# GpSimd's sums of exponentials and its low parts of q and k, issued as two instructions each instead of one

## The chip, the cores and the metric

The kernel runs on one core of one Trainium2 chip. Times are device microseconds of one launch; the kernel before has a median of 662.14 us over three runs (657.9, 662.14 and 665.37 us). The engines are called PE (TensorE), DVE (VectorE), ACT (ScalarE), POOL (GpSimd) and SP (SyncE).

## The reference, cut to what matters

Three layers follow one another: attention in which a query sees only the keys of its own cluster, a mixture of experts with two experts per token, and a soft mixture of experts. The change touches the first.

```python
def _attn_ref(q, k, v, centroids):          # q, k, v: (2, 8, 768, 64)
    ...
    mask = q_assign[:, :, :, None] == k_assign[:, :, None, :]
    scores = scale * np.matmul(q, k.transpose(0, 1, 3, 2))
    scores = np.where(mask, scores, -1000000000.0)
    scores = scores - np.max(scores, axis=-1, keepdims=True)
    attn = np.exp(scores)
    attn = attn / (np.sum(attn, axis=-1, keepdims=True) + 1e-09)
    return np.matmul(attn, v).astype(np.float32)

def reference(**kwargs):
    attn_out = _attn_ref(**attn_kwargs)
    x = np.ascontiguousarray(attn_out.transpose(0, 2, 1, 3)).reshape(B * S, H * D)
    x = _moe_ref(x=x, **moe_kwargs)
    return _moe2_ref(x=x, **moe2_kwargs)
```

## The kernel before, in words

**Pairs and steps.** The 16 heads are worked off as 8 pairs (p = 0 to 7), the two heads of a pair side by side. A pair has 12 steps: two halves of the 768 queries (qh), and for each six blocks of 128 keys (kc). Step (p, t) has qh = t // 6 and kc = t % 6. `score` (L363) makes the scores of 128 keys against 384 queries for both heads in a PSUM tile `psc` of two buffers, and ACT writes their exponentials to a tile `pt` (128 x 2 x 384, L375) of which there are five buffers. `av` (L378) multiplies `pt` with the values into `pav`.

**The sums of exponentials.** The denominators need the sum of the six `pt` tiles of one (p, qh). `add` (L388) gives it out: POOL sums the first n tiles into `psa` (n = 6 in pair 0, 4 in pairs 1 to 5, 3 in pairs 6 and 7), DVE sums the others into `psb`. The first sum reads two `pt` tiles (L402), each later one reads `psa` or `psb` and one `pt` tile (L405). One instruction covers 128 partitions x 768 elements. `total` (L407) adds `psb` to `psa` on DVE for the first three pairs (L411), `den` (L424) sums over the partitions on PE (`pden`), and DVE takes the reciprocals. A `pt` buffer is free for a later step when `av` and the sum have read it.

**High and low parts.** q and k are split into a high part in fp32r and a low part, and the scores are two matmuls, one on the high parts with the mask rows (`BK`, `BQ`) and one on the mixed parts (`AK`, `AQ`). ACT writes the high parts (`hk`, `hq`, `ak`, `aq`), POOL the low parts: `akl` (L301) once for each head, `aql` (L310) once for each half of the queries, 64 partitions x 768 elements each.

**Row maxima.** Before pair p is scored, `munit` (L317) computes its score tiles on PE into `pmx` (two buffers of PSUM) and DVE reduces each to row maxima `mp` (L336, L341); `mfin` (L343) gathers them.

**What sets the order.** `body` walks the steps two at a time and issues, in this order, what the tables `pre`, `mid` and `post` hold for a step: munits and the scores, the high parts, `av` and `add`, then the low parts, the cluster masks (`masks`, L222; L228 is its comparison on DVE), `total`, `den` and `xout` (L441). Between them `gap` issues the routing of finished tokens to the experts: chains of small DVE instructions on tiles of 128 x 48 or 128 x 24 (all under L563, the line of a helper) and then, on POOL, indirect DMAs that scatter token rows to `xg` in memory (L631). Towards the end of attention the first weights of the experts are split too, on DVE (L832) and POOL (L834), and their first tokens (L895). Each engine works its instructions off in the order in which they were issued.

**The other layers** (from about 255 us on) use POOL for scatters and splits of their own and are not touched by the change.

Of the kernel before, what the change touches and what calls it, by code (L numbers as in the profile page):

```python
# [12 lines left out]
OP = mybir.AluOpType  # L13
# [3 lines left out]
B, H, S, D = 2, 8, 768, 64  # L17
# [62 lines left out]
f32 = lambda t: t.bitcast(F32)  # L80


class Attention:
# [216 lines left out]

    def akl(self, p, hh):  # L301
        i = p % 2
        self.nc.gpsimd.tensor_tensor(self.AK[i][0:64, hh], self.raws[p][1][0:64, hh],
                                     f32(self.BK[i])[0:64, hh], op=OP.subtract)

    def aq(self, p, qh):
        q = self.raws[p][0][0:64].rearrange("p h (t n) -> p h t n", t=2)[:, :, qh]
# [2 lines left out]
    def aql(self, p, qh):  # L310
        i = p % 2
        q = self.raws[p][0][0:64].rearrange("p h (t n) -> p h t n", t=2)[:, :, qh]
        self.nc.gpsimd.tensor_tensor(self.AQ[i][64:128, qh], q, f32(self.BQ[i])[0:64, qh], op=OP.subtract)

    MU = 9

# [71 lines left out]
    def add(self, p, t):  # L388

        qh, kc = divmod(t, 6)  # L390
        pt = self.ptile
        n = 6 if p == 0 else 4 if p < MASKED else 3
        first = 0 if kc < n else n
        if kc == first:
            return
        eng = self.nc.vector if first else self.nc.gpsimd
        if kc == first + 1:
            k = "b" if first else "a"
            s = (self.g.at if first else self.g.xp).tile([128, 2, 384], F32, name=f"ps{k}", tag=f"ps{k}",
                                                         bufs=1 if first else 2)  # L400
            self.stile[p, qh, k] = s
            eng.tensor_tensor(s, pt.pop((p, t - 1)), pt.pop((p, t)), op=OP.add)  # L402
        else:
            s = self.stile[p, qh, "b" if first else "a"]
            eng.tensor_tensor(s, s, pt.pop((p, t)), op=OP.add)  # L405

    def total(self, p, qh):  # L407
        if (p, qh, "b") not in self.stile or p >= TWO:
# [1277 lines left out]
```

## Time and profile before

| | us |
|---|---|
| median of 3 runs | 662.14 |
| lowest and highest run | 657.9, 665.37 |
| profiled execution, its own time | 660.52 |
| its span, first to last instruction | 658.7 |
| PE busy | 623.3 (95%) |
| DVE busy | 414.6 (63%) |
| ACT busy | 312.4 (47%) |
| POOL busy | 292.6 (44%) |

The span is 1.8 us shorter than the execution's own time, and that execution lies 1.6 us under the median. Starts in the trace are counted from the span's start. In a row of a timeline a number in square brackets is how long the engine stood idle just before, and behind the arrow stands whose end it waited for. An instruction's duration includes the time for which it was held after its start.

### The profile page before, as it was taken

What the parts mean: (1) busy time and instruction counts of PE and PEld (TensorE: products, weight loads), DVE (VectorE), ACT (ScalarE), POOL (GpSimd) and SP (SyncE); (2) the same over time, 40 slices, a digit from 0 to 9 for tenths busy, and PEclk for the clock granted to TensorE, in tenths of its full rate; (3) what the DMA queues carried; (4) which work ended last, traced back from release to release, by engine and by line L of the source; (5) the groups of instructions that cost most, each with busy time, mean ns of one, the idle gap of its engine ahead of it and who ended that gap; (6) DMA issues with size and microseconds to landing.
All of it is one profiled execution on the core that took longest, in us unless ns stands there. A gap on an engine that the chain in (4) does not pass through costs nothing. (4 is left out here: it accounts for less than half of the span.)

```text
span 658.7 us, 10980 instructions
## 1 busy us (share of the span) xinstructions
PE 623.3 (95%) x3957; PEld 478.9 (73%) x3957; DVE 414.6 (63%) x872; ACT 312.4 (47%) x445; POOL 292.6 (44%) x256
## 2 busy tenths in 40 slices
PE   7899999999798999796999999999999999997996
PEld 5566666676565667685888888888888898885544
DVE  6777889779775698855655455454454556645633
ACT  5577585665457472343334334343434446543102
POOL 4899586864668792582123133251323403101100
PEclk9599999999799999987999999999999999999999
DMA  8393754836436413478574829969796758998995
GB/s 312 76 263 116 250 177 138 282 119 212 147 135 234 130 65 129 161 220 220 129 190 112 221 97 271 314 206 240 284 278 261 163 179 249 348 313 284 378 392 194
DMA packets 63098, 139.80 MB, mean 212 GB/s; under 512 B 15232, under 2 KB 30912, under 8 KB 60992
## 3 DMA queue, kind: packets, MB, share of 16 engines
q1 hardware_dynamic: 57040, 125.38, 56.9%
q0 software_dynamic: 6000, 13.68, 9.5%
q8 instruction: 32, 0.52, 0.3%
q14 instruction: 26, 0.21, 0.1%
HBM read 108.25 MB, written 28.68 MB: 208 GB/s over the span
## 5 line engine op out<-in xcount | busy, mean ns | idle before, releaser
L967 PE MATMUL py<-ring,H 128*128 128x512 f32 (+1 forms) x686 | 175.1, 400 | 6.1 <-DVE H L935 6.1
L832 DVE TENSOR_TENSOR ring<-wr,ring 128x1024 fp32r<-128x1024 f32 (+1 forms) x77 | 92.4, 1200 | 100.3 <-ACT ring L825 99.3
L967 PEld LDWEIGHTS py<-ring,H 128*128 128x128 f32 (+1 forms) x686 | 126.3, 188 | 33.1 <-DVE H L935 6.7
L825 ACT ACTIVATE ring<-wr 128x1024 fp32r<-128x1024 f32 x77 | 81.5, 1058 | 94.5 <-PE py L967 86.4
L375 ACT ACTIVATE pt<-psc 128x768 f32<-128x768 f32 x96 | 77.2, 810 | 71.0 <-PE psc L372 65.1
L975 POOL DMA_INDIRECT x2acc<-y,mdi x31 | 49.9, 1609 | 103.8 <-ACT y L999 98.0
L385 PE MATMUL pav<-pt,vt 128*64 128x384 f32 x384 | 75.2, 514 | 0.0
L336 DVE TENSOR_REDUCE mp<-pmx 128x1 f32<-128x512 f32 x96 | 63.2, 675 | 17.7 <-PE pmx L331 16.9
L932 ACT ACTIVATE H<-ph 128x256 fp32r<-128x256 f32 (+3 forms) x80 | 37.5, 468 | 71.9 <-PE ph L926 66.3
L926 PE MATMUL ph<-XS1a,ring 128*128 128x448 f32 (+2 forms) x288 | 70.4, 335 | 0.0
L926 PE MATMUL ph<-XS0a,ring 128*128 128x448 f32 (+3 forms) x252 | 64.6, 337 | 1.6 <-DVE ring L832 1.4
L405 POOL TENSOR_TENSOR psa<-psa,pt 128x768 f32<-128x768 f32 x32 | 62.0, 1936 | 3.5 <-ACT pt L375 1.4
L935 DVE SCALAR_TENSOR_TENSOR H<-ph,H 128x384 fp32r<-128x384 f32 (+1 forms) x120 | 44.4, 397 | 21.8 <-ACT H L932 20.2
L926 PEld LDWEIGHTS ph<-XS1a,ring 128*128 128x128 f32 x288 | 48.7, 189 | 4.0
L926 PE MATMUL ph<-XS0b,ring 128*128 128x256 f32 (+3 forms) x192 | 48.3, 329 | 0.0
L926 PEld LDWEIGHTS ph<-XS0a,ring 128*128 128x128 f32 x252 | 43.4, 188 | 6.3 <-DVE ring L832 1.9
L926 PE MATMUL ph<-XS1b,ring 128*128 128x256 f32 (+2 forms) x192 | 47.6, 322 | 0.3 <-DVE XS1b L895 0.3
L895 POOL TENSOR_TENSOR XS0b<-xr,XS0a 128x512 fp32r<-128x512 f32 (+1 forms) x9 | 16.8, 1871 | 64.5 <-ACT XS0a L889 64.5
L385 PEld LDWEIGHTS pav<-pt,vt 128*64 128x64 f32 x384 | 23.9, 139 | 25.6 <-issue 20.4
L331 PE MATMUL pmx<-even 96*128 96x512 f32 (+1 forms) x96 | 34.6, 420 | 5.4 <-DVE mp L336 4.5
L631 POOL DMA_INDIRECT xg<-x,idx x24 | 27.2, 1133 | 23.6 <-DVE inv L563 17.8
L341 DVE TENSOR_REDUCE mp<-pmx 128x2 f32<-128x512 f32 x48 | 32.9, 688 | 5.4 <-PE pmx L331 5.0
(335 smaller groups left out, 1030.8 us busy)
## 6 DMA issues: line engine op xcount, KB each, us to landing
wr<-in_w SPq DMA_DIRECT2D x80, 512.0 KB
v<-in_v SPq DMA_DIRECT2D x9, 2048.0 KB
xg<-xr SPq DMA_DIRECT2D x14, 512.0 KB
wr<-in_qk SPq DMA_DIRECT2D x8, 768.0 KB
early<-in_q SPq DMA_DIRECT2D x8, 768.0 KB
early<-in_k SPq DMA_DIRECT2D x8, 768.0 KB
x2acc<-xr SPq DMA_DIRECT2D x8, 512.0 KB
vt<-in_v SPq DMA_DIRECT2D x8, 384.0 KB
```

The lines of the kernel that those rows point to most:

```text
L331: nc.tensor.matmul(o, self.BQ[i][:96, qh, hh, 128 * c:128 * c + 128], self.BK[i][:96, hh, ks], start=True, stop=True)
L336: nc.vector.tensor_reduce(mp[:, 0, col:col + 1], ps, axis=AX.X, op=OP.max)
L375: nc.scalar.activation(pt, ps[:, :, :384], AF.Exp, scale=SCALE)
L385: nc.tensor.matmul(self.avp[p, qh][64 * hh:64 * hh + 64, :384], self.vt[p][:, hh, kc, :], pt[:, hh, :], start=(kc == 0), stop=(kc == 5))
L405: eng.tensor_tensor(s, s, pt.pop((p, t)), op=OP.add)
L825: self.nc.scalar.activation(self.ring[s][0], self.wr[s], AF.Copy)
L832: nc.vector.tensor_tensor(lo[:, :n], wr[:, :n], f32(hi)[:, :n], op=OP.subtract)
L926: nc.tensor.matmul(ph[:, :n], a[:, 128 * c:128 * c + 128], x[:, c, :], start=(c == 0 and i == 0), stop=(c == 3 and i == 2))
L932: nc.scalar.activation(HH, ph[:, :n], AF.Relu)
L935: nc.vector.scalar_tensor_tensor(o, ph[:, a:b], 0.0, f32(HH)[:, a:b], op0=OP.max, op1=OP.subtract)
L967: nc.tensor.matmul(o, x, y, start=(f == 0 and i == 0), stop=(f == NF - 1 and i == 2))
L975: st = nc.gpsimd.indirect_dma_start(out=out, out_offset=bass.IndirectOffsetOnAxis(ap=di, axis=0), in_=y, in_offset=None, compute_op=OP.add)
```

## The change

Every POOL instruction of the three functions is issued as two of half the length. A sum into `psa` is one instruction for each head (128 x 384), where it was one for both. `aql` is likewise one for each head (64 x 384). `akl`, which was for one head already, is cut at key 384. DVE's sums into `psb` stay whole. The sums have a line of their own afterwards, L414; the low parts are L305 and L316.

```diff
     def akl(self, p, hh):
         i = p % 2
-        self.nc.gpsimd.tensor_tensor(self.AK[i][0:64, hh], self.raws[p][1][0:64, hh],
-                                     f32(self.BK[i])[0:64, hh], op=OP.subtract)
+        for n in range(0, S, 384):
+            c = slice(n, n + 384)
+            self.nc.gpsimd.tensor_tensor(self.AK[i][0:64, hh, c], self.raws[p][1][0:64, hh, c],
+                                         f32(self.BK[i])[0:64, hh, c], op=OP.subtract)
...
     def aql(self, p, qh):
...
-        self.nc.gpsimd.tensor_tensor(self.AQ[i][64:128, qh], q, f32(self.BQ[i])[0:64, qh], op=OP.subtract)
+        for h in range(2):
+            self.nc.gpsimd.tensor_tensor(self.AQ[i][64:128, qh, h], q[:, h], f32(self.BQ[i])[0:64, qh, h], op=OP.subtract)
...
             self.stile[p, qh, k] = s
-            eng.tensor_tensor(s, pt.pop((p, t - 1)), pt.pop((p, t)), op=OP.add)
+            x, y = pt.pop((p, t - 1)), pt.pop((p, t))
         else:
             s = self.stile[p, qh, "b" if first else "a"]
-            eng.tensor_tensor(s, s, pt.pop((p, t)), op=OP.add)
+            x, y = s, pt.pop((p, t))
+        if first:
+            eng.tensor_tensor(s, x, y, op=OP.add)
+        else:
+
+            for hh in range(2):
+                eng.tensor_tensor(s[:, hh], x[:, hh], y[:, hh], op=OP.add)
```

On POOL, the stretch from the end of pair 4 into pair 5, ahead of the first scatter, stood like this before (`even`, `odda` and `oddb` hold the split q and k, `early` the loaded ones):

```order
L303 TENSOR_TENSOR even<-early,even 64x768
L402 TENSOR_TENSOR psa<-pt 128x768
L405 TENSOR_TENSOR psa<-psa,pt 128x768 x2
L303 TENSOR_TENSOR even<-early,even 64x768
L313 TENSOR_TENSOR even<-early,even 64x768 x2
L631 DMA xg<-x,idx 3712x516
```

And so it stands now:

```order
L305 TENSOR_TENSOR even<-early,even 64x384 x2
L414 TENSOR_TENSOR psa<-pt 128x384 x2
L414 TENSOR_TENSOR psa<-psa,pt 128x384 x4
L305 TENSOR_TENSOR even<-early,even 64x384 x2
L316 TENSOR_TENSOR even<-early,even 64x384 x4
L640 DMA xg<-x,idx 3712x516
```

Each instruction has become two next to each other, and nothing has moved past anything else. The second place is POOL's stretch with the scatters of the first batch, pairs 5 and 6. Before:

```order
L402 TENSOR_TENSOR psa<-pt 128x768
L631 DMA xg<-x,idx 3712x516 x4
L405 TENSOR_TENSOR psa<-psa,pt 128x768
L303 TENSOR_TENSOR odda<-early,oddb 64x768
L631 DMA xg<-x,idx 3712x516 x2
L313 TENSOR_TENSOR odda<-early,oddb 64x768 x2
L402 TENSOR_TENSOR psa<-pt 128x768
L405 TENSOR_TENSOR psa<-psa,pt 128x768
```

Now:

```order
L414 TENSOR_TENSOR psa<-pt 128x384 x2
L640 DMA xg<-x,idx 3712x516 x4
L414 TENSOR_TENSOR psa<-psa,pt 128x384 x2
L305 TENSOR_TENSOR odda<-early,oddb 64x384 x2
L640 DMA xg<-x,idx 3712x516 x2
L316 TENSOR_TENSOR odda<-early,oddb 64x384 x4
L414 TENSOR_TENSOR psa<-pt 128x384 x2
L414 TENSOR_TENSOR psa<-psa,pt 128x384 x2
```

Here too every scatter keeps its place between the sums. The order on PE, DVE, ACT and SP is that of before.

## Rows read from the trace of the kernel before

**Rows 1.** Windows: length, busy PE, PEld, DVE, ACT, POOL, granted clock, DMA share, GB/s

```profile
28.40:55.00 26.60, 25.58 (x155) 17.13 (x147) 19.88 (x34) 16.99 (x24) 25.84 (x14) 0.95 0.76 198
55.00:160.00 105.00, 104.39 (x701) 69.57 (x703) 83.81 (x162) 69.59 (x98) 75.44 (x41) 1.00 0.57 195
...
187.00:224.00 37.00, 34.70 (x238) 22.86 (x240) 22.50 (x47) 19.95 (x26) 33.38 (x24) 0.95 0.50 174
```

**Rows 2.** Waits up to 270 us, exponentials: total us, times, longest

```profile
ACT pt L375 <- PE psc L372: 65.1, 57, 3.2
```

**Rows 3.** Timeline of PE: instructions before which it stood idle

```profile
171.57 0.80 PE L331 MATMUL pmx<-even 96*128 96x256 f32 x2 [3.35 <-DVE mp L336]
...
211.94 0.62 PE L331 MATMUL pmx<-oddb 96*128 96x256 f32 x2 [1.84 <-DVE mp L336]
...
244.74 0.46 PE L432 MATMUL pden<-psb,sel 128*32 128x96 f32 x12 [0.54 <-DVE psb L405]
...
274.26 1.45 PE L926 MATMUL ph<-XS0a,ring 128*128 128x256 f32 x10 [1.44 <-DVE ring L832]
```

**Rows 4.** Timeline of DVE around the longest of these, and one undisturbed instruction

```profile
164.79 2.49 DVE L402 TENSOR_TENSOR psb<-pt 128x768 f32<-128x768 f32 x1
...
168.37 0.67 DVE L563 TENSOR_TENSOR ohe<-xr 128x48 f32<-128x48 f32 x1
...
169.29 1.63 DVE L563 SCALAR_TENSOR_TENSOR xr<-ohe,xr 128x48 f32<-128x48 f32 x1
170.84 0.68 DVE L336 TENSOR_REDUCE mp<-pmx 128x1 f32<-128x512 f32 x1
...
178.34 0.20 DVE L563 TENSOR_TENSOR ohe<-xr 128x48 f32<-128x48 f32 x1
```

**Rows 5.** DVE's first sums of a half: min/median/max ns, first and last start

```profile
L402 DVE TENSOR_TENSOR psb<-pt x14: 943/948/2489, 68.5 to 252.9; 128x768 f32<-128x768 f32 x14
```

**Rows 6.** Timeline of POOL beside the DVE rows of group 4

```profile
164.61 1.84 POOL L303 TENSOR_TENSOR even<-early,even 64x768 fp32r<-64x768 f32 x1 [5.36 <-ACT even L292]
166.41 2.56 POOL L402 TENSOR_TENSOR psa<-pt 128x768 f32<-128x768 f32 x1
169.05 3.68 POOL L405 TENSOR_TENSOR psa<-psa,pt 128x768 f32<-128x768 f32 x2
```

**Rows 7.** Timeline of POOL: undisturbed two-input instructions of 16 and 512 elements

```profile
25.25 0.22 POOL L502 TENSOR_TENSOR lim<-ebase,ecap 128x16 f32<-128x16 f32 x1
...
233.21 1.29 POOL L895 TENSOR_TENSOR XS0a<-xr,XS0a 128x512 fp32r<-128x512 f32 x1 [0.92 <-ACT XS0a L889]
```

**Rows 8.** Timeline of POOL and of DVE at 32 to 38 us

```profile
32.12 3.73 POOL L405 TENSOR_TENSOR psa<-psa,pt 128x768 f32<-128x768 f32 x2
35.80 2.16 POOL L303 TENSOR_TENSOR odda<-early,oddb 64x768 fp32r<-64x768 f32 x1
...
34.82 1.44 DVE L228 TENSOR_TENSOR xr<-xr 128x384 bf16<-128x384 f32 x1
```

**Rows 9.** Windows after three of PE's waits; columns as in rows 1

```profile
171.60:178.00 6.40, 6.40 (x19) 4.00 (x20) 4.33 (x10) 1.40 (x3) 4.72 (x3) 0.50 0.69 216
...
212.00:216.50 4.50, 4.50 (x17) 2.28 (x18) 3.00 (x4) 2.28 (x4) 3.96 (x4) 0.62 0.92 373
...
274.30:275.70 1.40, 1.40 (x10) 1.20 (x10) 1.35 (x5) 0.00 (x0) 1.15 (x2) 1.00 0.78 313
```

**Rows 10.** Timelines at 241 to 245 us: DVE, POOL

```profile
242.29 2.39 DVE L405 TENSOR_TENSOR psb<-psb,pt 128x768 f32<-128x768 f32 x1
...
241.33 2.53 POOL L402 TENSOR_TENSOR psa<-pt 128x768 f32<-128x768 f32 x1
```

**Rows 11.** Timelines at the end of pair 6: POOL, ACT, PE

```profile
220.05 1.83 POOL L402 TENSOR_TENSOR psa<-pt 128x768 f32<-128x768 f32 x1
...
222.39 0.81 ACT L375 ACTIVATE pt<-psc 128x768 f32<-128x768 f32 x1 [0.21 <-PE psc L372]
...
225.96 0.34 PE L370 MATMUL psc<-oddb 97*128 97x384 f32 x1
```

## The prediction

> **What bounds the kernel now.** I read the windows by stage first. From 28 us on PE is busy almost without a break while attention runs, 104.39 of the 105 us from 55 to 160 us, and POOL, whose instructions the change touches, is not the bound: 75.44 of the same 105 us. Two stretches differ. From 28.4 to 55 us POOL is busy 25.84 of 26.6 us, and from 187 to 224 us, where it also issues scatters, 33.38 of 37 us [rows 1]. The waits come second: the exponentials wait for the scores, 57 times and 65.1 us, so ACT follows PE and POOL's sums hold it up hardly anywhere [rows 2]. So POOL may take longer in most of attention at no cost, and what can be won is PE's idle time. I looked that up in PE's timeline, third. There are few places, and the longest is one wait of 3.35 us before 171.57 us, for a reduction of row maxima on DVE [rows 3].
>
> Fourth, I asked why DVE was late there. Its sum psb at 164.79 us took 2.49 us, and the undisturbed one takes 0.95 [rows 4, 5]. Two routing instructions of 48 elements took 0.67 and 1.63 us, where one took 0.20 us at 178.34. That is 1.54 + 0.47 + 1.43 = 3.4 us of being held, and straight behind the last comes the reduction at 170.84 that PE waits for [rows 4]. Each of them starts while a POOL instruction runs and ends just behind that instruction's end: POOL's L303 ends at 166.45, its first sum at 168.97, the first of the two L405 half-way through its 3.68 us, at about 170.9 [rows 6]. So a DVE instruction with two inputs in SBUF is held until the whole POOL instruction is over, and POOL is held by DVE in turn: the sum at 166.41 took 2.56 us in place of about 1.84.
>
> **The change part by part.** 48 sums and 32 low parts on POOL become 160 instructions of half the length. That does three things: each costs its fixed time once more, a DVE instruction waits at most half as long for POOL, and POOL can be stopped in the middle of what was one instruction.
>
> *Fixed time.* Two-input instructions of 16 and 512 elements took 0.22 and 1.29 us [rows 7], which is 2.16 ns an element on a fixed part of 0.19 us; 768 elements should then take 1.84 us, which is what L303 took [rows 6]. 384 elements come to 1.02 us, two of them to 2.03, so each split adds 0.19 us. 80 splits add 15 us to POOL. In the stretch up to 55 us there are 14 of them, 2.7 us, where only 0.8 us are free, so POOL enters pair 1 about 2 us late. Pairs 1 to 4, with 29.6 us free up to 160 us, take that up, and ACT, which waited for scores and not for POOL, has no reason to notice. I cost this at nothing.
> [...] By the elements alone the splits would be free and the sum below would be 0.7 us lower; the 16-element row says they are not.
>
> From 187 to 224 us, 11 instructions that run there are split, 2.1 us. The spare time is read at the end of that stretch: the sum at 220.05 frees a buffer at 221.88, the exponential that takes that buffer starts at 222.39, ends at 223.20, and PE needs the PSUM tile that it has read at 225.96 [rows 11]. That is 0.5 + 2.76 = 3.3 us, more than 2.1. But PE itself comes late there, after a wait of 1.84 us before 211.94 [rows 3] and 4.5 us at a mean clock of 0.62 [rows 9], which costs another 1.7 us. If PE were not late, nothing would be spare and up to 2.1 us would show. Value +0.7 us, a third of that, bounds 0 and +2.2.
>
> *The long wait.* I put halves of 1.02 us into the rows at 164 to 171 us. L303's first half ends at 165.6, so psb goes on 0.8 us earlier. Its second half then waits for psb, and the sum behind it starts about 1 us later than now, so the 48-element comparison that now starts at 168.37 still meets it, at 167.5, and ends at 168.5 in place of 169.04. The next one, now released at 170.85, is released by the end of a half at about 169.5. The reduction is 1.3 us earlier. If DVE arrives at psb only 0.2 us sooner (it was held in the same way before), psb slips in ahead of L303 altogether, and the gain is 2.0 us. Value −1.7 us; bounds −0.5 (psb's share alone, with half of it lost again to the later sums) and −3.35 (the whole wait).
>
> *The clock behind it.* [...] The wait that I expect, 3.35 − 1.7 = 1.65 us, lies between the one that left the clock alone and the one that did not, so I take half: −1.6 us, bounds 0 and −3.2.
>
> *Smaller waits.* The psb instruction at 242.29, held by the POOL sum that ran from 241.33 to 243.86, delayed PE by 0.54 us [rows 3, 10]. With halves DVE is let in about 0.7 us earlier. Value −0.5, bounds 0 and −1.0 for this and shorter ones of its kind. The waits from 260 us on have other causes, the routing chain and POOL's unsplit L834, and stay.
>
> *Sum:* −1.7 − 1.6 − 0.5 + 0.7 = −3.1 us on the profiled execution's 660.5, so 657.4. That execution is 1.6 us under the median of the runs, and I take the same difference off the median: 662.1 − 3.1 = 659.0 us. The bounds add up to −0.5 + 2.2 = +1.7 us and −3.35 − 3.2 − 1.0 = −7.6 us, so 663.8 and 654.5 us.
>
> **The rivals.**
>
> *The wait goes and the clock stays.* If DVE loses so little time that PE waits 1.44 us or less, the 3.2 us come back whole, and with 2 to 3.35 us of the wait: −2.7 − 3.2 − 1.0 + 0.4 = −6.5, so 655.6 us; the pure bound is 654.5. For it: DVE was held in the same way several times between 150 and 175 us, and each of these is shortened. Against it: the rows as I replay them leave 1.3 to 2 us of the wait.
>
> *POOL becomes the bound from 187 to 224 us* (the other side). POOL's sums give back the exponentials' buffers, and once they are later than 3.3 us against now, or PE comes sooner by as much, PE waits for scores that wait for ACT. The price is the 2.1 us of splits, a PE wait of the kind after which the clock fell, 4.5 × 0.38 = 1.7 us, and what POOL loses to DVE between its halves: the sum at 166.41 lost 0.7 us that way [rows 6], three such are 2.1 us. Less 1.7 us from the long wait and nothing else won: 662.1 + 2.1 + 1.7 + 2.1 − 1.7 = 666.3 us. It decides as soon as POOL's lag at 220 us passes 3.3 us. For it: 33.38 of 37 us [rows 1]. Against it: it needs lag of nearly twice the splits' own cost.
> [...]
>
> *The split does not do what it says.* POOL's second half has no wait in front of it and might follow so closely that DVE does not get between. Then DVE is held as long as now, and only the fixed time is left: 662.1 + 0.7 = 662.8 us. Against it: POOL's L303 started at 35.80, before its forerunner's end at 35.85, and took 2.16 us, 0.32 more than undisturbed, while the DVE comparison that had been held since 34.82 ended at 36.26 [rows 8]. DVE got in between two instructions that touched.
>
> **How the numbers follow.** The forecast, 659 us, has a chance of 0.42; the kept clock, 655.6 us, 0.28; POOL as the bound, 666.3 us, 0.17; no effect, 662.8 us, 0.13. The three runs of before lie 1.1% apart, and about 1% is what a measurement of this kernel can tell from no change; 1% is 6.6 us, so faster means under 655.5 and slower over 668.8. Half of the kept-clock cases and a few of the forecast's lie below 655.5, and cases in which the routing chain happens to meet POOL less often: 0.32. A third of POOL as the bound, with new waits behind it, lies above 668.8, and a little for other things: 0.08. The rest, 0.60, is within 1%. The range is 653.5 to 666.0 us: the lower end is the lower bound less 1 us for the spread of runs, the upper one the upper bound, 663.8, and on to the place of the rival on the other side. The likeliest case alone has 656 to 662.
>
> **What would show it.** A POOL half should take 1.0 us, and POOL's busy time should grow by 12 to 18 us. The psb instruction near 164.8 us and the routing instructions behind it should be held by 1.0 us at most, never 1.5. PE's wait before the row-maxima matmul near 170 us should be 1 to 2 us. I am wrong if that wait is as long as before or has moved, if DVE's two-input instructions are still held by 1.4 us and more, or if ACT's exponentials in pairs 5 to 7 wait for POOL by more than 2 us in all.

## The result, and the profile after

The changed kernel takes 665.35 us in the median of 20 runs (663.43 to 673.27), the kernel before 660.36 us in 20 runs beside it (657.67 to 665.37). The ratio is 1.010, with a 95% interval of 1.0071 to 1.0129: the change makes the kernel 1.0% slower, where I had forecast 0.5% faster. Thirteen of the changed kernel's runs lie between 663.4 and 667.1 us and seven between 669.9 and 673.3; no trace of the second group was taken, so what parts the two is open. The profiled execution took 665.38 us, with a span of 663.6 us, 4.9 us more than before.

The page's first part, busy time by engine:

```profile
PE 624.2 (94%) x3957; PEld 481.4 (73%) x3957; DVE 413.4 (62%) x872; ACT 312.0 (47%) x445; POOL 303.1 (46%) x336
```

PE's busy time grew by 0.9 us (623.3 before), its span by 4.9 us. So 4.0 of the 4.9 us are, on balance, time in which PE stood idle. POOL has its 80 instructions more and is busy 10.5 us longer. The windows by stage, columns as in [rows 1], say where:

```profile
28.40:55.00 26.60, 25.26 (x157) 16.42 (x151) 20.62 (x34) 16.86 (x24) 25.96 (x27) 0.98 0.75 197
55.00:160.00 105.00, 100.16 (x668) 67.43 (x668) 80.16 (x152) 66.66 (x93) 78.63 (x78) 0.98 0.54 180
160.00:187.00 27.00, 23.44 (x184) 15.80 (x182) 24.32 (x60) 14.95 (x24) 15.79 (x16) 0.94 0.57 195
187.00:224.00 37.00, 34.32 (x232) 23.68 (x231) 23.73 (x54) 21.35 (x29) 32.42 (x32) 0.95 0.46 163
```

The stretch that I had left out of the account, 55 to 160 us, went from 104.39 us of busy PE to 100.16. The stretch with the scatters, where I had feared for POOL, is as before (POOL 32.42 us, 33.38 before). PE's timeline, instructions before which it stood idle (the answer to [rows 3]):

```profile
91.98 0.50 PE L334 MATMUL pmx<-oddb 96*128 96x256 f32 x2 [2.41 <-DVE mp L339]
...
120.95 0.50 PE L334 MATMUL pmx<-even 96*128 96x256 f32 x2 [2.43 <-DVE mp L339]
...
173.40 0.50 PE L334 MATMUL pmx<-even 96*128 96x256 f32 x2 [1.05 <-DVE mp L339]
...
178.13 0.50 PE L334 MATMUL pmx<-even 96*128 96x512 f32 x1 [2.52 <-DVE mp L339]
...
215.57 0.50 PE L334 MATMUL pmx<-oddb 96*128 96x256 f32 x2 [2.10 <-DVE mp L339]
```

The wait of 3.35 us before 171.57 us has become 1.05 us, as I had expected. But there are three new waits of 2.4 to 2.5 us, all for row maxima on DVE. DVE's timeline tells why it was late (the answer to [rows 4]):

```profile
86.63 4.70 DVE L420 TENSOR_TENSOR psa<-psa,psb 128x768 f32<-128x768 f32 x1
91.25 1.27 DVE L339 TENSOR_REDUCE mp<-pmx 128x1 f32<-128x512 f32 x2
...
115.59 4.71 DVE L420 TENSOR_TENSOR psa<-psa,psb 128x768 f32<-128x768 f32 x1
...
168.91 0.95 DVE L410 TENSOR_TENSOR psb<-pt 128x768 f32<-128x768 f32 x1
...
171.21 0.57 DVE L572 TENSOR_TENSOR ohe<-xr 128x48 f32<-128x48 f32 x1
...
172.03 0.72 DVE L572 SCALAR_TENSOR_TENSOR xr<-ohe,xr 128x48 f32<-128x48 f32 x1
...
173.27 4.22 DVE L572 TENSOR_SCALAR x<-xr 128x6 f32<-128x6 f32 x1
```

The instructions that I had looked at are relieved: psb takes 0.95 us (2.49 before), the two routing instructions 0.57 and 0.72 (0.67 and 1.63). Two others are held far longer than anything was before: `total`, the addition of psb to psa (L420), takes 4.70 us twice, and a routing instruction on 6 elements 4.22 us. In the trace of before all four totals took 2.45 to 2.56 us, and PE did not wait behind them for more than 0.2 us. What POOL does meanwhile:

```profile
82.76 1.97 POOL L305 TENSOR_TENSOR odda<-early,oddb 64x384 fp32r<-64x384 f32 x2 [4.92 <-ACT oddb L292]
84.69 1.97 POOL L414 TENSOR_TENSOR psa<-pt 128x384 f32<-128x384 f32 x2
86.62 3.89 POOL L414 TENSOR_TENSOR psa<-psa,pt 128x384 f32<-128x384 f32 x4
90.47 2.67 POOL L305 TENSOR_TENSOR odda<-early,oddb 64x384 fp32r<-64x384 f32 x2
...
171.67 1.96 POOL L414 TENSOR_TENSOR psa<-pt 128x384 f32<-128x384 f32 x2
173.60 3.85 POOL L414 TENSOR_TENSOR psa<-psa,pt 128x384 f32<-128x384 f32 x4
```

The total that DVE starts at 86.63 is there for all four halves of 86.62 to 90.51 and is let in only when L305 begins, which it holds up in turn (2.67 us for two, 1.97 undisturbed). It passed three ends of instructions without getting in. The routing instruction at 173.27 began in the second half of its row and passed four. Before, the first of these places stood like this on POOL and then on DVE:

```profile
84.94 1.82 POOL L402 TENSOR_TENSOR psa<-pt 128x768 f32<-128x768 f32 x1
86.84 4.33 POOL L405 TENSOR_TENSOR psa<-psa,pt 128x768 f32<-128x768 f32 x2
...
87.04 2.45 DVE L411 TENSOR_TENSOR psa<-psa,psb 128x768 f32<-128x768 f32 x1
```

One sum ends at 86.76 and the next starts at 86.84: each sum continues the accumulator of the one directly before it and must wait for it, which leaves a pause of 0.08 us. The total of 87.04 got in at the first such pause that it met, behind the end of that sum. In the changed kernel a half continues what the half *two* before it wrote, and a half of 0.97 us (3.89 / 4) lies between. So halves follow each other with no pause at all: by their rows the two halves from 84.69 end at 86.66, and the next one starts at 86.62.

Comparing the start of the same matmuls in both traces gives the ledger. The changed kernel is level at 55 us, 1.8 us late at 92 and 3.8 at 121. Behind the second wait the granted clock is 0.57 for 4 us, which takes the lag to 5.3 us at 125:

```profile
121.00:125.00 4.00, 4.00 (x27) 1.66 (x28) 1.25 (x3) 0.17 (x1) 3.08 (x4) 0.57 0.97 306
```

It is 4.2 us at 168. The shortened wait brings it back to 0.6 us at 175, and the new one takes it to 3.0 us at 178. At 267 us, in the next layer, 2.1 us are left. The rest of the 4.8 us by which it is late at the end comes in layers that the change does not touch: 1.5 us near 310 us, and 1.0 us near 608 us, where PE ran at a lower granted clock than in the trace of before. The 6.7 us behind the same wait, before and then now:

```profile
602.64:609.34 6.70, 6.04 (x128) 4.53 (x128) 3.72 (x17) 3.27 (x8) 0.00 (x0) 1.00 1.03 418
...
606.35:613.05 6.70, 6.55 (x107) 5.42 (x110) 2.82 (x11) 2.59 (x6) 0.00 (x0) 0.75 1.02 415
```

The traces of the nine other whole kernels below have 0.53 to 0.75 there, so the trace of before is the exception, and nothing shows that the sums cause this part. The ratios above rest on all runs and not on this ledger.

### The profile page after: what moved, and what is told of

Same layout as the page of the kernel before. It is cut to its first block, busy times and chain, and to the rows that moved or that the text cites. A ratio compares the mean times of both kernels' runs of the same rounds, so it can differ in the third digit from the quotient of the medians.

```text
span 663.6 us, 11063 instructions
## 1 busy us (share of the span) xinstructions
PE 624.2 (94%) x3957; PEld 481.4 (73%) x3957; DVE 413.4 (62%) x872; ACT 312.0 (47%) x445; POOL 303.1 (46%) x336
## 5 line engine op out<-in xcount | busy, mean ns | idle before, releaser
L841 DVE TENSOR_TENSOR ring<-wr,ring 128x1024 fp32r<-128x1024 f32 (+1 forms) x77 | 90.5, 1175 | 102.3 <-ACT ring L834 101.3
L378 ACT ACTIVATE pt<-psc 128x768 f32<-128x768 f32 x96 | 77.4, 811 | 75.7 <-PE psc L375 65.3
L414 POOL TENSOR_TENSOR psa<-psa,pt 128x384 f32<-128x384 f32 x64 | 65.1, 1046 | 1.1 <-ACT pt L378 1.1
L334 PE MATMUL pmx<-oddb 96*128 96x512 f32 (+1 forms) x96 | 31.9, 376 | 5.2 <-DVE mp L339 4.5
```

The lines of the kernel that those rows point to most:

```text
L334: nc.tensor.matmul(o, self.BQ[i][:96, qh, hh, 128 * c:128 * c + 128], self.BK[i][:96, hh, ks], start=True, stop=True)
L378: nc.scalar.activation(pt, ps[:, :, :384], AF.Exp, scale=SCALE)
L414: eng.tensor_tensor(s[:, hh], x[:, hh], y[:, hh], op=OP.add)
L841: nc.vector.tensor_tensor(lo[:, :n], wr[:, :n], f32(hi)[:, :n], op=OP.subtract)
```

## The experiments

My first theory: a row of halves without a pause shuts DVE out, and the three holds are the whole loss. The rival: the loss is POOL's fixed time for 80 more instructions. The first four runs (before: 661.06 us, 17 runs) change the order, take each half of the change alone, and put the row by itself.

**Head by head.** The halves of the two steps that `body` issues together are put in order of heads, so that a half continues what the half directly before it wrote.

```diff
-            for hh in range(2):
-                eng.tensor_tensor(s[:, hh], x[:, hh], y[:, hh], op=OP.add)
+            return [lambda hh=hh: eng.tensor_tensor(s[:, hh], x[:, hh], y[:, hh], op=OP.add) for hh in range(2)]
...
+            for hh in range(2):
+                for f in halves:
+                    if f:
+                        f[hh]()
```

> The same halves as in the change, but the two sums of a double step are issued head by head (a of step 1, a of step 2, b of step 1, b of step 2), so that every other half waits for the one directly before it and POOL pauses there. Theory A (DVE is shut out while halves of sums follow one another without a pause, and that makes the loss): no two-input DVE instruction is held for more than two halves, the sums psa<-psa,psb on DVE take 3.0 us at most instead of 4.7, PE's waits of 2.4 us near 90 and 119 us go, and the time is 655 to 660 us. Theory B (the loss is POOL's 10 to 15 us of added fixed time): nothing changes, 664 to 667 us.

Measured: 652.71 us (6 runs), ratio 0.9896 (0.9862 to 0.9929). The same number of instructions on POOL is now 1.0% faster than before, so fixed time is not the loss. The time lies even under the range of theory A. The waits near 90 and 120 us are gone, and the totals (shortest, median and longest in ns) took 0.95 to 1.82 us:

```profile
L419 DVE TENSOR_TENSOR psa<-psa,psb x4: 949/1596/1817, 69.9 to 109.7; 128x768 f32<-128x768 f32 x4
```

**Low parts alone halved**, sums whole.

> Only the low parts of q and k are halved, the sums of exponentials are whole. Theory A: no DVE instruction is held over several POOL instructions, 657 to 661 us. Theory B: two fifths of the added fixed time and so of the loss, about 662 us.

Measured: 659.85 us (12 runs), ratio 0.9985 (0.9966 to 1.0004). No difference; the wait of 3.4 us near 170 us stays.

**Sums alone halved**, low parts whole.

> Only the sums of exponentials are halved, the low parts are whole. Theory A: the DVE sums psa<-psa,psb are held over four halves again (4.5 us and more, twice), 664 to 667 us. Theory B: three fifths of the loss, about 663 us, and no instruction held so long.

Measured: 666.92 us (6 runs), ratio 1.0092 (1.0065 to 1.0119). The whole loss is in the sums. The wait near 170 us is 5.67 us long there. DVE and PE at the first held total:

```profile
86.47 4.57 DVE L417 TENSOR_TENSOR psa<-psa,psb 128x768 f32<-128x768 f32 x1
...
91.70 0.50 PE L331 MATMUL pmx<-oddb 96*128 96x256 f32 x2 [2.28 <-DVE mp L336]
```

**Rows by themselves.** Only rows of eight POOL instructions of one form, and a 48-element DVE instruction against each at six phases.

> No part of the computation: POOL runs rows of eight two-input instructions (halves of one accumulator in turn; a chain on one half; halves in turn into a fresh output; low parts on 64 partitions; whole tiles into two outputs in turn), and one DVE instruction of 48 elements with two inputs starts at six different moments of each row. Theory A: in the chain DVE is let in at the first end of a POOL instruction, within 1.0 us; in the rows without pauses it waits for two ends or more, up to the whole row of 8 us. If it is let in at the first end everywhere, the long holds have another cause.

Measured: DVE was let in at the first end in all 30 rows, those of low parts alone too; the longest hold made it 1.14 us. (It always began in one of the first two instructions behind a wait.) So halves without a pause do not shut DVE out by themselves, and my theory was wrong or not whole. Something else in the kernel had to take part. In the changed kernel the rows that shut DVE out all stood behind `akl`, whose instructions (L305) run on partitions 0 to 63 alone, while the sums run on all 128. New theory, which none of these rows shows by itself: after an instruction on 64 partitions, the part of POOL that had nothing to do runs ahead of the other, and as long as no pause brings them together, some part of POOL is inside an instruction at every moment.

The next four runs (before: 660.6 us, 23 runs, one of them 2063.55 us) test that.

**Rows behind other instructions.** Eight halves without a pause, behind two instructions of four kinds.

```python
for h in range(2):
    if form == "low":
        TT(low[0:64, h], st[0:64, h], src[0:64, h], op=OP.subtract)
    elif form == "cross":
        TT(low[64:128, h], st[0:64, h], src[0:64, h], op=OP.subtract)
    else:
        TT(alt[:, h], st[:, h], src[:, h], op=OP.add)
for k in range(8):
    h = k % 2
    TT(t[:, h], t[:, h], src[:, h], op=OP.add)
```

> A probe that leaves out all computation of the three layers and only issues rows of GpSimd instructions, with a 48-element VectorE instruction issued against each row at six phases. Every row ends with eight halves (128 x 384) added in place to one accumulator without a pause. Ahead of the eight stand, by row: two low parts on partitions 0 to 63 (low); two that read 0 to 63 and write 64 to 127 (cross); two halves on all 128 partitions (first); the same with another accumulator (other). Theory (after an instruction on 64 partitions one part of GpSimd runs ahead of the other, so that in a row without pause some part of it is always inside an instruction): in the rows low the VectorE instruction is held over two and more ends, 2 us and longer; in first and other it is let in at the first end, 1.1 us at most; cross as low or as first, not decided. Rival (the position of the buffer, or what else runs in the whole kernel): all rows let it in at the first end.

DVE's timeline, three of the instructions against rows behind low parts, then one against a row behind halves on 128 partitions:

```profile
35.33 0.34 DVE L113 TENSOR_TENSOR w<-u,v 128x48 f32<-128x48 f32 x1
...
46.73 6.73 DVE L113 TENSOR_TENSOR w<-u,v 128x48 f32<-128x48 f32 x1
...
58.13 6.48 DVE L113 TENSOR_TENSOR w<-u,v 128x48 f32<-128x48 f32 x1
...
181.62 1.03 DVE L113 TENSOR_TENSOR w<-u,v 128x48 f32<-128x48 f32 x1
```

And POOL's rows that belong to the second and to the last of these:

```profile
43.85 1.94 POOL L97 TENSOR_TENSOR low<-st,src 64x384 fp32r<-64x384 f32 x2 [1.60 <-DVE st L109]
45.76 7.64 POOL L104 TENSOR_TENSOR acc<-acc,src 128x384 f32<-128x384 f32 x8
...
178.74 1.95 POOL L101 TENSOR_TENSOR alt<-st,src 128x384 f32<-128x384 f32 x2 [1.60 <-DVE st L109]
180.65 4.79 POOL L104 TENSOR_TENSOR acc<-acc,src 128x384 f32<-128x384 f32 x5
```

The instruction, 0.14 us where no row ran beside it, took 6.73 us: it ended at 53.46, just behind the row's end at 53.40, and was let in nowhere before. The second of the kind ended with its row too. Behind halves on 128 partitions, and behind low parts that write partitions 64 to 127, the longest took 1.05 us. Two other phases behind low parts (0.60 us and the 0.34 above) met the first half of the eight and were let in at its end; the last two met no row. So low parts on partitions 0 to 63 ahead of the row are what was missing, and the shutting begins with the second half of the row. The changed kernel's row at 171.67 agrees: the instruction of 172.03 was let in at the end of the first half, that of 173.27 not before the row's end. Why the first half does not shut, no run tells.

**No total.** The two held totals are taken away: TensorE sums psa and psb one after the other, as for the later pairs.

```diff
-TWO = 3
+TWO = 0
```

> The changed kernel with TWO = 0: VectorE's three totals psa + psb are not made, TensorE sums psa and psb one after the other in den (the pairs 3 to 7 do so anyway). Theory (what was lost is the two totals near 87 and 116 us, held over four halves each, and the two TensorE waits of 2.4 us behind them): both waits go, the time falls by 4 to 6 us to about 660 us, level with the same edit of the kernel before. Rival (the loss is GpSimd's fixed time of the 80 splits): the time stays 663 to 666 us, 4 to 5 us over the same edit of the kernel before.

> The kernel before with TWO = 0, the control for the run above: no TensorE wait stood behind its totals (0.95 to 2.6 us each), so both theories expect 660 to 663 us, the extra TensorE work of the dens included.

Measured: the changed kernel without totals 658.5 us (12 runs), ratio 0.9968 (0.9946 to 0.9989); the kernel before without them 661.39 us (12 runs), ratio 1.002 (0.9996 to 1.0044). (The traces have four totals, of pairs 1 and 2; the expectation counts three.) With no totals to hold, the change wins 2.9 us where it had lost 5.0; the theory had the two level. The waits near 90 and 120 us are gone; the third new wait, whose DVE instruction is not a total, stands in PE's timeline as before:

```profile
171.21 0.51 PE L334 MATMUL pmx<-even 96*128 96x512 f32 x1 [2.51 <-DVE mp L339]
```

**Heads in turn.** The halves of every other step in the opposite order, so that every second half must wait for the one directly before it.

```diff
-            for hh in range(2):
+            for hh in (0, 1) if t % 2 else (1, 0):
```

> The changed kernel with the two halves of every other step's sum in the opposite order (head 1 first), so that every second half continues the accumulator that the half directly before it wrote, and must wait for its end. Same instructions, same count. Theory (VectorE is kept out only where halves follow without a pause, and a wait on the instruction directly before makes one): the totals near 87 and 116 us are held over at most two halves, 0.95 to 2.7 us in place of 4.7, the TensorE waits of 2.4 us behind them go, and the time is 652 to 659 us. Rival (what made the head-by-head order fast is another arrangement of the steps, such as sums that come later, and not the pause): totals of 4 us and more remain and the time stays 663 to 666 us.

Measured: 652.49 us (6 runs), ratio 0.9876 (0.9844 to 0.9909). The totals took 0.95 to 1.55 us. The timelines at the first of the two places (POOL, then DVE) and of the wait near 170 us (PE):

```profile
83.20 1.97 POOL L414 TENSOR_TENSOR psa<-pt 128x384 f32<-128x384 f32 x2
85.25 4.72 POOL L414 TENSOR_TENSOR psa<-psa,pt 128x384 f32<-128x384 f32 x4
...
85.13 0.95 DVE L420 TENSOR_TENSOR psa<-psa,psb 128x768 f32<-128x768 f32 x1
...
165.08 0.50 PE L334 MATMUL pmx<-even 96*128 96x256 f32 x2 [1.05 <-DVE mp L339]
```

And the window of the stage around that wait:

```profile
160.00:187.00 27.00, 25.37 (x199) 17.49 (x196) 22.60 (x60) 16.55 (x25) 22.44 (x22) 1.00 0.51 172
```

POOL pauses from 85.17 to 85.25, and the total slips in. The granted clock of the stage is 1.00.

**A pause behind the low parts** (this and the next two: before 660.5 us, 13 runs). The halves stay as in the change, without pauses; only behind each L305 stand two tiny instructions that wait for it.

```diff
+        z = self.g.xp.tile([128, 1], F32, name="zz", tag="zz", bufs=2)
+        self.nc.gpsimd.tensor_copy(z[0:64], f32(self.AK[i])[0:64, hh, S - 1:S])
+        self.nc.gpsimd.memset(z, 0.0)
```

> The changed kernel with its halves in their own order (head 0, head 1), and two one-column instructions on GpSimd behind the low parts of k: a copy of the last column that the low part wrote, which must wait for its end, and a memset of 128 partitions that must wait for the copy. Theory (the row is shut to VectorE because it follows low parts on 64 partitions without a pause, as in the probe's rows low): with the pause in between, the totals near 87 and 116 us are let in at the first or second end, 0.95 to 2.0 us, the waits of 2.4 us behind them go, and the time is 653 to 660 us, although GpSimd has some 32 instructions more. Rival (the missing pauses within the sums are enough by themselves): totals of 4 us and more remain and the time is 664 us and more.

Measured: 653.49 us (6 runs), ratio 0.9891 (0.9847 to 0.9936), with 32 instructions more than the change. POOL at both places, then DVE:

```profile
82.64 0.18 POOL L308 COPY zz<-odda 64x1 f32<-64x1 f32 x1
82.88 0.10 POOL L309 MEMSET zz<- 128x1 f32 x1
82.97 1.97 POOL L417 TENSOR_TENSOR psa<-pt 128x384 f32<-128x384 f32 x2
84.89 4.62 POOL L417 TENSOR_TENSOR psa<-psa,pt 128x384 f32<-128x384 f32 x4
...
164.90 3.90 POOL L417 TENSOR_TENSOR psa<-psa,pt 128x384 f32<-128x384 f32 x4
...
84.48 1.28 DVE L423 TENSOR_TENSOR psa<-psa,psb 128x768 f32<-128x768 f32 x1
...
165.22 1.67 DVE L575 TENSOR_TENSOR xr<-xr 128x48 f32<-128x48 f32 x2
...
167.41 0.50 DVE L575 TENSOR_TENSOR xr<-xr,iode 128x48 f32<-128x48 f32 x1
```

The four halves from 164.90 still follow without a pause, and DVE gets in at the ends of three of them in a row: the two instructions of 165.22 and the one of 167.41 end by 165.96, 166.89 and 167.91, where the halves end by 165.89, 166.86 and 167.84. In the change the same row kept DVE out to its end. So it is the low parts on 64 partitions directly ahead, and not the missing pauses alone. Whether the pause or the memset on 128 partitions opens the row, the run does not part.

**Heads in turn, low parts whole.**

> Sums in halves with the opposite head order on every other step, low parts whole as before. Theory (the sums' halves are what lets VectorE in earlier; the low parts' halves give little, as when they alone were cut): 653 to 657 us, level with the same order beside halved low parts (652.5) or a little above. Rival (both splits are needed, since VectorE meets the low parts as often): half of the gain is gone, 656 us and more.

Measured: 654.86 us (8 runs), ratio 0.9904 (0.9871 to 0.9937). The sums carry most of the gain; halved low parts beside them are worth some 2 us by the medians (654.86 against 652.49), which is not shown, since the intervals overlap.

**Heads in turn, no total.**

> The opposite head order on every other step together with TWO = 0. The two edits remove the same loss in two ways, so they should not add up: TensorE's longer dens (0.8 us by the control) against three totals that cost TensorE nothing now. Theory: 651 to 655 us, no better than the head order alone. Rival (totals still cost something): under 650 us.

Measured: 654.19 us (6 runs), ratio 0.9894 (0.9852 to 0.9937). The two edits do not add up, so once DVE is let in, no gain is left to see at the totals.

The versions head by head, heads in turn, and with a pause behind the low parts take 1.0 to 1.2% less than the kernel before, with intervals clear of 1, and 1.8 to 1.9% less than the change; their intervals overlap, and none is shown to be the best.

## Why the prediction was wrong

**The step that failed** is the premise that "a DVE instruction waits at most half as long for POOL", and with it the dismissal of the rival "the split does not do what it says". I wrote that DVE "got in between two instructions that touched", from [rows 8], and took that for every end of a half. The second instruction of that boundary was a low part. At the boundary that decided, from one in-place half to the next behind a low part, the trace of before had no example, because its whole sums wait for each other. The rival also had the wrong size: I priced it at "held as long as now", 662.8 us. As soon as four halves count as one, a hold grows from 1.5 us (2.45 − 0.95) to 3.75 us (4.70 − 0.95), which is longer than before the split. My own sign of being wrong, two-input instructions still held by 1.4 us and more, came true. Even the comparison of [rows 8], my only evidence, was then held for longer, 2.63 us as against 1.44, to the end of a row of halves behind low parts (DVE, then POOL):

```profile
34.43 2.63 DVE L228 TENSOR_TENSOR xr<-xr 128x384 bf16<-128x384 f32 x1
...
32.77 3.87 POOL L414 TENSOR_TENSOR psa<-psa,pt 128x384 f32<-128x384 f32 x4
36.61 2.26 POOL L305 TENSOR_TENSOR odda<-early,oddb 64x384 fp32r<-64x384 f32 x2
```

**Where the holds fell** I had not asked. I followed the DVE instructions that were late before, and not the totals, which were held by 1.5 us then with cover to spare. PE's row maxima follow directly behind them. With 2.2 us more, the cover was gone and PE waited 2.41 and 2.43 us. Without totals the change is 6.9 us faster (665.35 against 658.5).

**The long wait, −1.7 us**, was right as far as it went. psb went in undisturbed, which was my "slips in ahead of L303 altogether", and the wait fell by 2.3 us to 1.05. Then the routing instruction at 173.27 met the shut row (1.32 us before, held too, which I had not counted), and 2.52 us came back. Together that is 3.57 us of waiting where there had been 3.35, so nothing of this term was left.

**The clock, −1.6 us**, was half of the 3.2 us that 6.4 us at a granted clock of 0.50 cost before [rows 9], and no run shows such a half behind a wait of 1.65 us. In its place, behind the waits of 1.05 and 2.52 us, the granted clock from 178 to 184.5 us was 0.74; that is 1.7 us lost against 3.2. So the size came out, but by luck: the clock fell behind the wait of 2.52 us, which the forecast did not have, and it fell behind the wait of 2.43 us before 120.95 us too (0.57 for 4 us, another 1.7 us lost). Nor did the length of the wait decide, as I had assumed: behind the wait of 2.41 us the granted clock was 1.00 from 92 to 96 us, and behind one of 1.51 us, in the version with a pause behind the low parts, 0.64 from 179.3 to 184 us. With the heads in turn and head by head, where 1.05 us of the long wait was left, the stage from 160 to 187 us stood at 1.00 (before 0.87, in the change and with the pause 0.94). So the rival "the wait goes and the clock stays" (655.6 us) comes near to what the change does once the rows are opened: 652.5 to 653.5 us.

**Smaller waits, −0.5 us**: PE's lag falls by 0.7 us between 240 and 247 us. Right.

**Fixed time and POOL's queue**: a half takes 1.00 us in the median, as worked out. POOL's busy time grew by 10.5 us, a little under my 12 to 18. The exponentials' waits are still for the scores:

```profile
ACT pt L378 <- PE psc L375: 65.3, 52, 5.0
```

That is 65.3 us as against 65.1 in [rows 2]. From 165 to 270 us they wait for POOL for 1.5 us in all, under the 2 us that I had named as a sign. With the heads in turn POOL is busy 85.14 us of the 105 from 55 to 160 us, and the kernel is faster. POOL as the bound, the rival that gave 666.3 us, came near to the measured time for a reason that was not so.

**What the faster versions give back**: the version with heads in turn is 11.9 us ahead of before at 267 us, and 8.1 at the end. Near 592 us a wait of 2.25 us has become 3.25, and the granted clock for the 6.7 us behind it is 0.56 (1.00 before), which is 2.9 us more. As the ledger says, the lower clock there stands in every trace but that of before, in the slower change too, so it is no price of being faster. This was read in one trace of each and not tried.

## What to carry to other kernels

Cutting a GpSimd instruction to let VectorE in earlier works only if VectorE is let in at the cut. Look at what stands ahead: behind low parts on partitions 0 to 63, GpSimd instructions that followed without a wait counted here as one (an addition of 0.95 us took 4.70, one of 0.14 us 6.73). Make each piece depend on the one directly before it (here a change of loop order alone was worth 12.9 us, 665.35 against 652.49), and follow every VectorE instruction that reads two tensors beside GpSimd, not only those that are late today.

## What the hardware showed

VectorE was locked out over seven GpSimd instructions in a row: 6.73 us for an instruction of 0.14 us behind two low parts on partitions 0 to 63, 1.05 us at most behind the other three kinds. A pause of some 0.08 us, made by a wait, opened the row.

Also a VectorE instruction on 6 elements that by its row reads one tensor, TENSOR_SCALAR at 173.27, was held (4.22 us; 1.32 before, 0.40 with the heads in turn), not only those with two. That parts of GpSimd run apart behind instructions on 64 partitions was my theory and was not shown: the profile has one span for an instruction. Why low parts that write partitions 64 to 127 do not shut the row (1.05 us at most) stays open.
